# A two-block transformer kernel with its opening rebuilt: load order, first v tiles by chunks, v one tile further ahead, VectorE operations interleaved

## The chip, the cores and the metric

The kernel runs on one core of a Trainium2 chip. The metric is the device time of one execution in microseconds (us). All runs compared here are of the fast state. TensorE is called PE below, VectorE DVE, ScalarE ACT, GpSimd POOL; SP is the engine that issues most DMAs.

## The reference

Both halves take bf16 inputs; x is 2048 x 640.

```python
# A: linear attention, 32 heads of 20
qkv = layernorm(x) @ wqkv
pq, pk = q @ w_phi[h], k @ w_phi[h]
phi_q = concat(softmax(pq), softmax(-pq)); phi_k = concat(softmax(pk), softmax(-pk))
kv = phi_k^T v;  z = sum_s phi_k
o  = (phi_q @ kv) / (phi_q . z + 1e-6)
h  = x + o @ wo
# B: gated FFN, F = 1536
out = h + (gelu(layernorm(h) @ w_gate) * (layernorm(h) @ w_up)) @ w_down
```

## The kernel before

The rows are 16 tiles of 128. The opening loads x and the weights, normalizes and transposes the first tiles, and folds w_phi into the k weights ("fold": `WkT` with the block diagonal `BD` gives `Wk2`). A loop over the 16 tiles follows: `pk` = k projection on PE, `E` = exp of it on ACT (both signs), `pv` = v projection of a later tile on PE, `vS` = its copy out of PSUM on ACT, then `sk` (sums of E) and `rs` (their reciprocals) on DVE, `vt` = vS times rs, one half on POOL and the other on DVE or POOL, and at last `kvp`, the sum over tiles of E^T vt, on PE. After the loop come q, attention and FFN. The program's order on each engine is the order of the code.

```python
# opening: loads
nc.scalar.dma_start(wphi, ...)
nc.sync.dma_start(x_sb[0][:, 0:1, :], ...); nc.sync.dma_start(x_sb[0][:, 1:2, :], ...)
for u in range(2):                                   # W_v in two column halves
    nc.sync.dma_start(Wv[:, :, u * HD:(u + 1) * HD], ...)
    nc.scalar.dma_start(x_sb[0][:, 2 + u:3 + u, :], ...)
nc.sync.dma_start_transpose(WkT, A_wqkv[:, D:2 * D])
nc.scalar.dma_start(x_sb[1], ...)
nc.sync.dma_start_transpose(WqT, A_wqkv[:, 0:D])
for dst, src in ((x_sb[2], ...), (x_sb[3], ...), (Wg, wg_v)):
    nc.sync.dma_start(dst, src)
...
def k_norm(t):
    nc.vector.reduce_sum(sk, Ek[t]...)
    nc.vector.reciprocal(rs, sk)
    for s, eng in ((1, nc.gpsimd), (0, nc.gpsimd if t in VP else nc.vector)):
        eng.tensor_tensor(vt[:, s], vS[t % 6], rs[...], ALU.mult)
...
for t in range(NT):
    if 6 <= t + 5 < NT: ln_ap(t + 5, on_act=True)    # LN1T by DMA transpose
    k_tile(t)
    ...
    if t + 3 < NT: v_tile(t + 3)
    if t % 2 == 1 and t + 7 < NT: ln_st(t + 7, t + 8)
    if t in FQ: fold(WqT, Wq2, True, [FQ.index(t)])
    k_norm(t)
    if t % 2 == 1 and t >= 5: kv_tile(t - 5); kv_tile(t - 4)
    if t == 10: nc.sync.dma_start(Wo, wo_v); nc.sync.dma_start(Wu, wu_v)
    ...                                              # at t == 15: four groups of q
for t in range(12, NT): kv_tile(t)
```

The softmax here doesn't subtract the row's maximum and nothing guards it: scores larger than these inputs give would overflow.

## Time and profile before

| | before |
|---|---|
| median time when the prediction was made | 286.35 us (285.9 to 286.82, 3 runs; a fourth later makes it 286.24) |
| span of the profiled run | 284.6 us |
| PE busy / DVE busy in the span | 273.3 / 170.6 us |
| last `kvp` ends | 76.66 us |
| from there to the end of the span | 207.9 us |

The last two rows split the program where the change stops: everything that it touches lies before the last `kvp`. That end is the row's start plus its length in PE's timeline (74.94 + 1.72). A row of a timeline has start and length in us, then the engine, the source line, the operation and its tiles; a bracket gives the idle time before it and what ended that. The table of stretches of the kernel before shows the same split. Its columns are the stretch, its length, then each engine's busy us (and instructions), the granted PE clock, the DMA share and GB/s:

```profile
0.00:76.59 76.59, 70.24 (x779) 47.40 (x781) 65.72 (x108) 54.27 (x79) 50.07 (x78) 1.00 0.61 152
76.59:284.60 208.01, 203.02 (x1539) 124.67 (x1549) 104.89 (x179) 87.40 (x149) 46.86 (x131) 1.00 0.19 45
```

The first busy figure is PE's, the second that of its weight loads, the third DVE's, then ACT's and POOL's. In the first stretch PE idles for 6.35 us and DVE for 10.9, of which 6.3 lie before the first `sk` and 2.2 behind the last `vt`; in the second PE idles for 5 us in 208.

### The profile page before, as it was taken

The numbers are of one execution on the slowest core, as the hardware profiler recorded it, in microseconds if no ns is written. First come the engines' busy times: TensorE is split into PE (matmuls) and PEld (weight loads), VectorE is DVE, ScalarE is ACT, GpSimd is POOL, SyncE is SP. The second block draws the span as 40 slices with busy tenths as digits, with TensorE's granted clock in tenths as the row PEclk, the third lists the DMA queues.
The fourth block names the chain that finished last, engine by engine and source line by source line (L and its number), as shares of the span: only waits on it lengthen the run. The fifth ranks groups of instructions, "written<-read, shape, count | busy, mean of one in ns | idle before, by whom it ended". The sixth has DMA issues, their size and how long they took to land.

```text
span 284.6 us, 5745 instructions
## 1 busy us (share of the span) xinstructions
PE 273.3 (96%) x2314; PEld 172.1 (60%) x2329; DVE 170.6 (60%) x287; ACT 141.7 (50%) x227; POOL 96.9 (34%) x209
## 2 busy tenths in 40 slices
PE   7798999899999999999999999999999999999995
PEld 2475677675545678778764454675455567444573
DVE  6679999999577685775522748522575732323222
ACT  2479777965887865545425454322436440132200
POOL 6226777797501123724312144220135330000000
PEclk9999999999999999999999999999999999999999
DMA  7999622480080011314210112232021313000011
GB/s 210 230 287 299 62 51 50 98 343 1 8 273 0 0 26 25 69 48 93 48 46 25 23 25 47 47 67 73 2 46 23 59 37 92 25 1 0 0 48 46
DMA packets 40971, 21.05 MB, mean 74 GB/s; under 512 B 33136, under 2 KB 39280, under 8 KB 40944
## 3 DMA queue, kind: packets, MB, share of 16 engines
q1 hardware_dynamic: 39856, 19.67, 28.4%
q10 hardware_dynamic: 1088, 1.01, 1.1%
q8 instruction: 18, 0.29, 0.4%
q14 instruction: 9, 0.07, 0.1%
HBM read 10.18 MB, written 2.62 MB: 45 GB/s over the span
## 4 chain that ended last, share of the span: by engine, by line
PE 77%; DVE 7%; DMA 6%; ACT 4%; POOL 3%; issue 3%; ACTq 0%; DVEq 0%; POOLq 0%
PE gu L517 34%; PE pd L532 18%; PE pq L310 8%; PE po L472 7%; DMA WkT<-in_A_wqkv_dram 4%; PE pk L243 4%; PE ab L412 2%; DVE sk L272 2%; ACT E L266 2%; PE kvp L288 2%; PE pv L243 1%; POOL vt L277 1%; DVE stats L105 1%; DMA oT<-o 1%; DMA wphi<-in_A_w_phi_dram 1%
## 5 line engine op out<-in xcount | busy, mean ns | idle before, releaser
L520 ACT ACTIVATE g<-gu 128x512 bf16<-128x512 f32 (+1 forms) x60 | 30.7, 512 | 73.7 <-PE gu L517 72.8
L523 DVE TENSOR_TENSOR GT<-gu,g 128x512 bf16<-128x512 f32 (+1 forms) x60 | 34.5, 581 | 54.2 <-ACT g L520 54.0
L517 PE MATMUL gu<-LN2T,Wg 128*128 128x512 bf16 (+1 forms) x289 | 61.3, 335 | 1.5 <-DVE GT L523 0.8
L517 PE MATMUL gu<-LN2T,Wu 128*128 128x512 bf16 (+1 forms) x300 | 61.7, 336 | 0.0
L532 PE MATMUL pd<-Wd,GT 128*128 128x320 bf16 x384 | 53.9, 299 | 0.0
L532 PEld LDWEIGHTS <-GT 128*128 128x128 bf16 x384 | 37.4, 98 | 15.7 <-DVE GT L523 0.9
L517 PEld LDWEIGHTS <-Wu 128*128 128x128 bf16 x300 | 29.3, 98 | 22.6
L517 PEld LDWEIGHTS <-Wg 128*128 128x128 bf16 x300 | 28.4, 98 | 21.7 <-issue 1.0
L243 PEld LDWEIGHTS <-LN1T 128*128 128x128 bf16 x320 | 30.6, 98 | 16.1 <-DMA LN1T<-ln 1.7
L277 POOL TENSOR_TENSOR vt<-vS,rs 128x672 bf16<-128x672 bf16 x22 | 34.1, 1570 | 7.4 <-DVE rs L274 6.2
L538 DVE TENSOR_TENSOR y<-pd,x_sb 128x640 bf16<-128x640 f32 (+1 forms) x17 | 13.3, 784 | 30.7 <-PE pd L532 30.7
L420 ACT COPY AB<-ab 128x704 f32<-128x704 f32 x28 | 19.6, 748 | 14.4 <-PE ab L412 14.2
L243 PE MATMUL pv<-Wv,LN1T 128*128 128x320 bf16 x160 | 24.2, 299 | 2.5 <-DMA LN1T<-ln 1.4
L243 PE MATMUL pk<-Wk,LN1T 128*128 128x320 bf16 x160 | 24.2, 299 | 1.1 <-ACT E L266 1.0
L472 PE MATMUL po<-Wo,oT 128*128 128x320 bf16 x160 | 24.4, 299 | 0.3 <-DMA oT<-o 0.3
L453 DVE TENSOR_TENSOR tt<-AB,w 128x1280 bf16<-128x1280 f32 x16 | 23.8, 1486 | 1.2 <-POOL w L446 0.9
L266 ACT ACTIVATE E<-pk 128x640 bf16<-128x640 f32 x32 | 20.7, 702 | 5.5 <-PE pk L243 5.4
L272 DVE TENSOR_REDUCE sk<-E 128x64 f32<-128x1280 bf16 x16 | 23.1, 1447 | 0.2 <-ACT E L266 0.2
L310 PE MATMUL pq<-LN1T,Wq 128*128 128x512 bf16 x96 | 22.7, 379 | 0.2
L315 ACT ACTIVATE Eq<-pq 128x1024 bf16<-128x1024 f32 (+1 forms) x22 | 19.4, 951 | 4.7 <-PE pq L310 4.7
L472 PEld LDWEIGHTS <-oT 128*128 128x128 bf16 x160 | 15.5, 98 | 7.7 <-DMA oT<-o 0.6
L495 POOL TENSOR_SCALAR v<-sm 128x1 f32<-128x1 f32 x14 | 8.4, 599 | 30.6 <-DVE x_sb L486 30.6
(76 smaller groups left out, 260.7 us busy)
## 6 DMA issues: line engine op xcount, KB each, us to landing
out_dram<-y SPq DMA_DIRECT2D x15, 160.0 KB, 1.8
Wg<-in_B_w_gate_dram SPq DMA_DIRECT2D x1, 1920.0 KB, 11.5
Wu<-in_B_w_up_dram SPq DMA_DIRECT2D x1, 1920.0 KB, 10.5
Wd<-in_B_w_down_dram SPq DMA_DIRECT2D x1, 1920.0 KB, 7.9
x_sb<-in_A_x_dram SPq DMA_DIRECT2D x2, 640.0 KB, 5.9
Wv<-in_A_wqkv_dram SPq DMA_DIRECT2D x2, 400.0 KB, 8.0
Wo<-in_A_wo_dram SPq DMA_DIRECT2D x1, 800.0 KB, 6.3
x_sb<-in_A_x_dram ACTq DMA_DIRECT2D x1, 640.0 KB, 8.3
```

Source lines behind the costliest of these rows:

```text
L243: nc.tensor.matmul(ps[:, u, 0:HD], lhsT=lnT(t, c), rhs=W[:, c, u * HD:(u + 1) * HD], start=(c == 0), stop=(c == NC - 1))
L266: nc.scalar.activation(Ek[t][:, s, :].rearrange("p (u f) -> p u f", u=2), pk[:, :, 0:HD], ACTF.Exp, scale=(1.0 if s == 0 else -1.0))
L272: nc.vector.reduce_sum(sk, Ek[t].rearrange("p s (h f) -> p (s h) f", f=Dh), axis=AX.X)
L277: eng.tensor_tensor(vt[:, s], vS[t % 6], rs[:, s * H:(s + 1) * H, None].to_broadcast([P, H, VC]), ALU.mult)
L310: nc.tensor.matmul(pqs[j][:, i, :], lhsT=Wq2[:, kc, c * P:(c + 1) * P], rhs=LN1T[b][:, kc, :], start=(kc == 0), stop=(kc == NC - 1))
L420: (nc.vector.tensor_copy if u >= 2 - dve else nc.scalar.copy)(AB[:, :, u * UH:(u + 1) * UH].rearrange("p s h f -> p s (h f)"), ab[u][:, :, ...
L453: nc.vector.tensor_tensor(tt.rearrange("p s (h f) -> p s h f", f=Dh), num, w[:, :, :, None].to_broadcast([P, 2, H, Dh]), ALU.mult)
L472: nc.tensor.matmul(po[:, u, 0:HD], lhsT=st[t][:, c, :], rhs=Wo[:, c, u * HD:(u + 1) * HD], start=(c == 0), stop=(c == NC - 1))
L517: nc.tensor.matmul(gu[:, i, 0:n], lhsT=W[:, c, f * P:(f + 1) * P], rhs=LN2T[b][:, c, a0:a1], start=(c == 0), stop=(c == NC - 1))
L520: nc.scalar.activation(g[:, 0:n], gu[:, 0, 0:n], ACTF.Gelu_apprx_tanh)
L523: nc.vector.tensor_tensor(st[b, "g", f][:, a0:a1], gu[:, 1, 0:n], g[:, 0:n], ALU.mult)
L532: nc.tensor.matmul(pd[:, u, 0:HD], lhsT=st[b, "g", f][:, tl * P:(tl + 1) * P], rhs=Wd[:, f, u * HD:(u + 1) * HD], start=(f == 0), stop=(f ...
```

## The change

The intent: x first, W_v in row chunks so that v can start chunk by chunk; one v tile more before the first k; the big W_gate load out of the opening; DVE operations interleaved so that dependent ones do not stand next to each other.

```diff
-    VP = (1, 3, 5, 7, 9, 11)
-    FQ = (8, 9, 10, 11, 12)
+    VP = (0, 2, 4, 6, 9, 11)          # tiles whose vt is POOL's alone
+    FQ = (4, 5, 6, 7, 8)              # where W_q is folded
+    WA, WB = 2,0                      # warm-ups, before 3 and 2
+    T3 = 3                            # until here PSUM has 4 buffers, then 3 and kvp
... ln_stats: all bn_stats first, then the bn_aggr ...
+    for t in range(4):
+        (nc.sync, nc.scalar)[t % 2].dma_start(x_sb[0][:, t:t + 1, :], x_v[:, t:t + 1, :])
     nc.scalar.dma_start(wphi, ...)
-    (x tiles, W_v in column halves)
+    for c in range(NC):
+        nc.sync.dma_start(Wv[:, c, :], w_v[:, c, 2 * D:3 * D])
+    for t in (0, 2):
+        nc.sync.dma_start(x_sb[1][:, t:t + 2, :], x_v[:, 4 + t:6 + t, :])
     nc.sync.dma_start_transpose(WkT, A_wqkv[:, D:2 * D])
... x_sb[2], WqT, x_sb[3]; Wg no longer here ...
     def k_norm(t):
         nc.vector.reduce_sum(sk, ...)
+        if t - 1 in todo:
+            todo.pop(t - 1)()          # the previous tile's vt on VectorE
         nc.vector.reciprocal(rs, sk)
+        mult(1, nc.gpsimd)
+        if t in VP:          mult(0, nc.gpsimd)
+        elif t == NT - 1:    mult(0, nc.vector)
+        else:                todo[t] = lambda: mult(0, nc.vector)
... v of tiles 0 and 1 by row chunks between the transposes; v of tile 3 around the fold ...
... a first Exp on ACT ahead of all data; LN1T of tile 4 copied by DVE; ln and q moved within the loop's pass ...
-        if t + 3 < NT:
-            v_tile(t + 3)
-        if t % 2 == 1 and t + 7 < NT:
-            ln_st(t + 7, t + 8)
+        if t + 4 < NT:
+            v_tile(t + 4)
+        if t % 2 == 0 and t + 8 < NT:
+            ln_st(t + 8, t + 9)
         if t == 10:
+            nc.sync.dma_start(Wg, wg_v)
             nc.sync.dma_start(Wo, wo_v)
             nc.sync.dma_start(Wu, wu_v)
```

## The prediction

> **What bounds the kernel now.** I read the page's busy line first, then the whole list of waits of TensorE (PE), then the timelines of PE, VectorE (DVE), ScalarE (ACT), GpSimd (POOL) and the SP queue over the first 77 us, because the change touches only that stretch.
>
> The page, busy time:
> ```profile
> PE 273.3 (96%) x2314; PEld 172.1 (60%) x2329; DVE 170.6 (60%) x287; ACT 141.7 (50%) x227; POOL 96.9 (34%) x209
> ```
> PE is busy for 273.3 of 284.6 us, so only 11.3 us of PE idle exist in the whole program. The list of PE's waits says where:
> ```profile
> PE pv L243 <- DMA LN1T<-ln: 1.4, 1, 1.4
> PE wu L189 <- DVE zero L174: 1.2, 1, 1.2
> PE pv L243 <- DMA Wv<-in_A_wqkv_dram: 1.1, 1, 1.1
> PE pk L243 <- ACT E L266: 1.0, 2, 0.8
> PE gu L517 <- DVE GT L523: 0.8, 2, 0.5
> PE wa L207 <- DMA WkT<-in_A_wqkv_dram: 0.6, 1, 0.6
> ```
> The columns are us in total, times, longest. Together with four shorter waits (0.4, 0.2, 0.2, 0.2 us) the opening and the k/v loop hold 6.3 us of it. The rest of the removable time is disguised as work: 15 warm-up matmuls (`wu`), whose rows begin at 1.24, 6.23 and 7.58 us.
>
> PE is not the only engine near its limit. DVE is 9.5 to 9.7 us busy in every 10 us from 20 to 60 us. Its timeline over one pair of k tiles:
> ```profile
> 32.44 1.43 DVE L272 TENSOR_REDUCE sk<-E 128x64 f32<-128x1280 bf16 x1
> 33.97 0.55 DVE L274 RECIPROCAL rs<-sk 128x64 f32<-128x64 f32 x1
> 34.44 1.43 DVE L272 TENSOR_REDUCE sk<-E 128x64 f32<-128x1280 bf16 x1
> 35.97 0.55 DVE L274 RECIPROCAL rs<-sk 128x64 f32<-128x64 f32 x1
> 36.56 1.42 DVE L277 TENSOR_TENSOR vt<-vS,rs 128x672 bf16<-128x672 bf16 x1
> 37.90 0.87 DVE L105 BATCH_NORM_STATS2 stats<-x_sb 128x6 f32<-128x320 bf16 x2
> 38.81 0.21 DVE L106 BATCH_NORM_AGGREGATE mv<-stats 128x2 f32<-128x12 f32 x1
> 38.93 0.83 DVE L105 BATCH_NORM_STATS2 stats<-x_sb 128x6 f32<-128x320 bf16 x2
> 39.80 0.21 DVE L106 BATCH_NORM_AGGREGATE mv<-stats 128x2 f32<-128x12 f32 x1
> 39.92 1.43 DVE L272 TENSOR_REDUCE sk<-E 128x64 f32<-128x1280 bf16 x1
> ```
> Columns: start, length. A pair costs DVE 39.92 - 32.44 = 7.48 us, while PE needs about 6.4 (the first pk of three successive pairs starts at 30.44, 36.85, 43.28). DVE therefore falls behind, and is excused at the end by four q groups that fill PE:
> ```profile
> 67.28 7.73 PE L310 MATMUL pq<-LN1T,Wq 128*128 128x512 bf16 x34
> 74.94 1.72 PE L288 MATMUL kvp<-vt,E 128*64 128x84 bf16 x80
> ```
> DVE's last `vt` begins at 73.53 for 0.86 (ends 74.39), POOL's last at 73.57 for 2.00 (ends 75.57); the last kv tile needs it near 76.2. So the slack of DVE and POOL against PE is only some 0.6 us. That is the reading the prediction rests on: PE cannot gain more than 0.6 us in the opening unless DVE also ends earlier. After 77 us (q groups, attention, FFN) the kernel runs on PE with 1.5 us of idle, and the change does not reorder it.
>
> **What the Trainium skill says.** (1) "TensorE: Matmul & The Clock Gate", Part 1: PE starts at half clock, and some 3.4 us of sustained matmuls release it. The trace agrees: the first ten warm-ups take 4.31 us (431 ns each), the three at 6.23 take 0.27 each start to start. So the first ten cannot go, the other five can. (2) "DMA: Bandwidth & Descriptors", Issuing engines are not separate DMA queues: SP and ACT share 16 DMA engines. The trace agrees: the DMA share is 1.05 from 2 to 9 us (306 GB/s) and 1.09 from 9 to 14.4 (182 GB/s). Moving loads between queues brings no bandwidth; only order changes. (3) The same page, Latency and other measured facts, gives DMA transposes a lower rate (261 GB/s) than plain loads. Here still lower: 182 GB/s where WkT dominates. (4) "VectorE: DVE Perf Modes", The DRAIN you can't avoid, says that a semaphore between chained ops costs nothing extra and that each op waits until the pipe empties. This trace differs: a dependent step starts 0.10 us after the op before ended (sk to rs), an independent one 0.08 us before it ended (rs to sk). That difference is what interleaving can recover.
>
> **The change part by part.**
>
> *Loads.* x tiles 0-3 first on both queues, then W_v in five row chunks, x[4..7] behind, then WkT. Before, the first v matmul waited for a whole column half of W_v until 9.31. Ahead of chunk 0 stand only 4x160+25 KB; at 306 GB/s from about 2 us that is 4.3 us, then 0.55 us for each chunk of 160 KB: all five by about 7.3, late issues included (loads reuse eight semaphores, so the fourth chunk is issued only when an x tile has landed). The 1.1 us wait for W_v goes, and v starts when LN1T of tile 0 is copied, about 7.4. WkT, however, still has the same bytes ahead of it (2.1 MB plain) and is now behind x[4..7] on its own queue: I estimate it lands at 14.5, as before (14.42).
>
> *Warm-ups.* 3+2 become 2+0: 3 x 0.27 = 0.8 us less.
>
> *PE to the fold.* Estimated: v parts of tiles 0 and 1 from 7.4 (0.136 us a matmul), a gap of 0.5 us at 9.0 for ln of tile 2, transposes of tiles 2 and 3, done about 11.2. Then a new wait: v of tile 2 takes the PSUM buffer of v of tile 0, whose copy stands on ACT behind the LN1T copy of tile 3 (tp at 10.65, copies 0.69 each): it starts near 12.45. v2 and half of v3 (2.0 us) end near 14.5, where WkT is there. Fold, with v3's second half inside, ends about 18.0, pk0 starts about 18.3 against 17.13. But v3 (1.36) and a transpose (0.28) more are done: net 0.5 us ahead.
>
> *Loop waits on PE.* The 1.35 us wait for the LN1T transpose at 29.07 stood behind Wg (1.9 MB, 11.5 us to landing) on the queue; Wg moves to tile 10, so it goes. The waits for E (1.0 us) came from ln late for DVE's stats; stats now run 8 tiles ahead: mostly gone. Sum on PE: 0.5 + 1.35 + 1.0 = 2.9 us at most.
>
> *DVE.* Removed: per pair, vt is put between sk and rs and the aggregates behind four stats. By the start-to-start steps above a pair becomes 1.35+1.34+0.47+1.53+0.47+1.99 = 7.15 against 7.48, and a late tile 2.65 against 3.0. Added: one ln (0.4) and one LN1T copy (0.5) move from ACT. Before the first sk, DVE now also does stats of tiles 8 and 9 (2.0 us), so sk0 comes at about 22.3 against 20.01, but those 2.0 us are missing later. Walking the new order from there gives the last vt at about 71.9 against 74.39: 2.5 us earlier.
>
> *v one tile further ahead.* vS still has six buffers, so evicting v of t+4 needs vt of t-2 (before: t+3 and t-3). vt of t ends about 8 us after pk of t begins, 2.5 PE tiles. So ACT will wait for POOL and DVE, and ACT frees PSUM: a new coupling. I charge it 1 us of PE between 28 and 52 us.
>
> Sum: PE alone 2.9 less 1.0 of coupling = 1.9; DVE allows 2.5. I take **2.0 us** at the last kv tile, and the rest of the program shifts by it: 286.35 - 2.0 = 284.3 us (0.7%).
>
> **Rivals.** (a) *DVE paces the loop completely*: with six vS buffers, ACT and then PE follow vt. For it: 7.15 us a pair on DVE, 7.9 with a W_q copy, against PE's 6.4. Then the gain is what PE keeps, 0 to 1 us: 285.4 to 286.3. (b) *All idle goes*, the coupling hides behind the three PSUM buffers and the fold is not late: gain 3 to 3.5 us, 282.9 to 283.4. Against it: DVE's 2.5 us. (c) *WkT lands later*, since x[4..7] is now ahead on its queue and the transpose's issue (7.70 us before) begins only about 5.4: at 16 us the fold is 1.5 us late and the gain shrinks to 0.5 us: 285.9. (d) *A large gain above 2%* needs 5.7 us out of 6.3 us idle and 0.8 us of warm-ups in this stretch, of which the first 1.2 us before any data and most of the x latency stay: almost excluded. Slower by 2% would need a new wait of that size with PE full: hardly.
>
> **Range and chances.** 284.3, with (a) and (c) on one side and (b) on the other: 282.5 to 286.1. Faster by over 2%: 0.03; within 2%: 0.96; slower: 0.01.
>
> **What would show it.** PE's waits after: none on W_v, none on LN1T's transpose; a PE gap of about 1.2 us ahead of v of tile 2 released by ACT's vS copy; fold start near 14.5; pk0 near 18.3. DVE: sk0 near 22.3, pairs near 7.15, last vt near 71.9, with rs no longer right behind its sk in even tiles. ACT: waits of vS copies on DVE or POOL vt, which did not exist before. The last kvp should end 2 us before 76.6, and the stretch from there to the end should keep its length. Wrong would be: WkT after 15.5, PE stalls in the loop of over 2 us, or a tail that changes by over 0.5 us because of Wg's later load.

## The result

| | before | after |
|---|---|---|
| median time | 286.24 us (285.9 to 286.82, 4 runs) | 284.09 us (283.92 to 284.17, 4 runs) |
| span of the profiled run | 284.6 | 282.2 |
| last `kvp` ends | 76.66 | 72.51 |
| from there to the end | 207.9 | 209.7 |

The ratio is 0.9922, 95% interval 0.9905 to 0.994, within 2%. Ratios are the mean time of one kernel's fast runs over that of the other's of the same rounds, so not quite the ratio of the medians.

The total came out as predicted, 2.2 us less. But its two parts did not: the touched stretch gained 4.15 us, not 2.0, and the untouched rest lost 1.75 us, which was predicted to keep its length. The stretches of the changed kernel:

```profile
0.00:72.44 72.44, 68.81 (x777) 46.67 (x777) 61.13 (x110) 53.11 (x78) 48.86 (x80) 1.00 0.60 160
72.44:282.20 209.76, 203.75 (x1553) 124.75 (x1549) 104.85 (x179) 87.14 (x148) 47.08 (x131) 1.00 0.19 45
```

In the first stretch PE's idle fell from 6.35 to 3.63 us (72.44 - 68.81) and its busy time by 1.43 us (fewer and faster warm-ups, mainly): together 4.15. DVE's busy time there fell by 4.6 us. In the second stretch DVE, ACT and POOL do the same work in the same busy time.

PE's waits in the changed kernel, to be read against those in the prediction (us in total, times, longest):

```profile
PE po L511 <- DMA oT<-o: 1.8, 1, 1.8
PE tp L136 <- POOL ve L110: 1.4, 1, 1.4
PE wu L194 <- DVE zero L179: 1.2, 1, 1.2
PE gu L556 <- DVE GT L562: 0.8, 2, 0.5
PE tp L136 <- DVE ln L128: 0.5, 2, 0.3
PE pk L248 <- ACT E L280: 0.3, 1, 0.3
```

The waits for LN1T, W_v, WkT and the casts of W_k are gone from the list, which leaves out gaps under 0.15 us, and of E's 1.0 us 0.3 stay. Two have grown: the first transpose waits for the statistics of the first x tile for 1.4 us (before 0.4), and one `po` of the attention waits 1.8 us for a DMA transpose of `oT` (before 0.3). The second one is far behind the change and is the lost time of the tail.

PE's timeline in the opening of the changed kernel:

```profile
6.58 0.45 PE L136 MATMUL tp<-ident,ln 128*128 128x128 bf16 x5 [1.42 <-POOL ve L110]
...
8.04 1.94 PE L264 MATMUL pv<-Wv,LN1T 128*128 128x320 bf16 x12
...
11.95 2.20 PE L248 MATMUL pv<-Wv,LN1T 128*128 128x320 bf16 x15
13.99 0.79 PE L212 MATMUL wa<-BD,WkT 128*128 128x140 bf16 x12
...
16.83 1.57 PE L248 MATMUL pk<-Wk,LN1T 128*128 128x320 bf16 x10
```

There is no gap ahead of v of tile 2 (11.95), the fold starts at 13.99 without waiting for WkT, and the first pk at 16.83, with v of tile 3 and one transpose more already done than before.

DVE's timeline over one pair of k tiles, the counterpart of the pair in the prediction:

```profile
26.53 1.43 DVE L287 TENSOR_REDUCE sk<-E 128x64 f32<-128x1280 bf16 x1
27.88 0.85 DVE L295 TENSOR_TENSOR vt<-vS,rs 128x672 bf16<-128x672 bf16 x1
28.64 0.55 DVE L291 RECIPROCAL rs<-sk 128x64 f32<-128x64 f32 x1
29.11 1.43 DVE L287 TENSOR_REDUCE sk<-E 128x64 f32<-128x1280 bf16 x1
30.64 0.55 DVE L291 RECIPROCAL rs<-sk 128x64 f32<-128x64 f32 x1
31.11 1.61 DVE L106 BATCH_NORM_STATS2 stats<-x_sb 128x6 f32<-128x320 bf16 x4
32.63 0.33 DVE L108 BATCH_NORM_AGGREGATE mv<-stats 128x2 f32<-128x12 f32 x2
32.87 1.43 DVE L287 TENSOR_REDUCE sk<-E 128x64 f32<-128x1280 bf16 x1
```

The pair takes 32.87 - 26.53 = 6.34 us instead of 7.48. From start to start, `vt` accounts for 0.58 us of this (1.34 to 0.76), the statistics with their aggregates for 0.26, and the order of `sk`, `rs` and `vt` for 0.30. The largest single difference is `vt`: 0.85 us instead of 1.42 for the same 128x672 multiplication. All ten of them, before and then after (min/median/max in ns):

```profile
L277 DVE TENSOR_TENSOR vt<-vS,rs x10: 858/1378/1515, 22.1 to 73.5; 128x672 bf16<-128x672 bf16 x10
```

```profile
L295 DVE TENSOR_TENSOR vt<-vS,rs x10: 847/854/935, 27.9 to 69.1; 128x672 bf16<-128x672 bf16 x10
```

Before, DVE's half (36.56 to 37.98 in the pair of the prediction) fell among POOL's three multiplications (34.67 to 39.14), and both engines were slowed. Now DVE's half comes one tile later; in the pair above (27.88 to 28.73) POOL is between two groups of `vt` (one ends at 26.71, the next starts at 29.34) and runs its small operations. POOL gains too: its 22 `vt` took 34.1 us before and 29.8 after. In the loop DVE even waits for ACT (3.2 us in five waits): it is no longer the engine that falls behind.

### The profile page after: what moved, and what is told of

Same layout as the page of the kernel before. It is cut to its first block, busy times and chain, and to the rows that moved or that the text cites. A ratio compares the mean times of both kernels' runs of the same rounds, so it can differ in the third digit from the quotient of the medians.

```text
span 282.2 us, 5752 instructions
## 1 busy us (share of the span) xinstructions
PE 272.6 (97%) x2326; PEld 171.4 (61%) x2326; DVE 166.0 (59%) x289; ACT 140.2 (50%) x226; POOL 95.9 (34%) x211
## 4 chain that ended last, share of the span: by engine, by line
PE 86%; DVE 5%; ACT 3%; DMA 3%; POOL 1%; issue 1%; ACTq 0%; POOLq 0%
PE gu L556 35%; PE pd L571 18%; PE pq L335 8%; PE po L511 7%; PE pk L248 7%; PE pv L248 5%; PE kvp L313 2%; PE ab L451 2%; DVE stats L106 2%; DMA oT<-o 2%; DMA x_sb<-in_A_x_dram 1%; DVE sk L287 1%; ACT E L280 1%; ACT Eq L340 1%; PE tp L136 1%
## 5 line engine op out<-in xcount | busy, mean ns | idle before, releaser
L248 PEld LDWEIGHTS <-LN1T 128*128 128x128 bf16 x300 | 28.5, 98 | 11.8 <-issue 0.7
L295 POOL TENSOR_TENSOR vt<-vS,rs 128x672 bf16<-128x672 bf16 x22 | 29.8, 1374 | 9.1 <-DVE rs L291 7.1
L248 PE MATMUL pv<-Wv,LN1T 128*128 128x320 bf16 x140 | 21.3, 299 | 0.0
```

Source lines behind the costliest of these rows:

```text
L248: nc.tensor.matmul(ps[:, u, 0:HD], lhsT=lnT(t, c), rhs=W[:, c, u * HD:(u + 1) * HD], start=(c == 0), stop=(c == NC - 1))
L295: eng.tensor_tensor(vt[:, s], vS[t % 6], rs[:, s * H:(s + 1) * H, None].to_broadcast([P, H, VC]), ALU.mult)
```

## The experiments

All times are medians; the end of the last kvp and the tail (from there to the end of the span) are from each run's profile. "Before" runs beside each kernel on the same chip.

| run | time | ratio to before | last kvp ends | tail | wait for oT |
|---|---|---|---|---|---|
| before | 286.24 | 1 | 76.66 | 207.9 | 0.3 |
| after | 284.09 | 0.9922 | 72.51 | 209.7 | 1.8 |
| b_wg | 286.2 | 0.9992 (0.9977 to 1.0007) | 77.05 | 207.9 | 0.3 |
| b_dve | 285.08 | 0.9965 (0.9946 to 0.9983) | 75.27 | 207.9 | 0.3 |
| b_dve_wg | 284.26 | 0.993 (0.9914 to 0.9947) | 74.17 | 208.3 | 0.7 |
| a_nodefer | 285.5 | 0.9978 (0.9966 to 0.9989) | 74.44 | 209.6 | 1.8 |
| a_wgearly | 289.67 | 1.0133 (1.0112 to 1.0154) | 76.85 | 209.6 | 1.7 |
| a_x0 | 284.14 | 0.9923 (0.9904 to 0.9943) | 72.54 | 209.7 | 1.8 |
| a_tiny3 | 284.48 | 0.994 (0.9924 to 0.9955) | 73.39 | 209.5 | 1.7 |
| a_tiny20 | 283.03 | 0.9887 (0.9864 to 0.991) | 72.96 | 207.8 | none |
| a_again | 284.02 | 0.9934 (0.992 to 0.9948) | 72.82 | 209.6 | 1.7 |
| a_tiny10 | 282.33 | 0.9865 (0.9852 to 0.9877) | 72.25 | 207.9 | none |
| a_wphi | 283.19 | 0.9902 (0.9887 to 0.9917) | 72.97 | 209.5 | 1.7 |
| a_best | 282.42 | 0.9871 (0.9857 to 0.9885) | 72.39 | 207.9 | none |

All gave correct results.

### Is PE's idle worth anything while DVE lags? (b_wg, b_dve, b_dve_wg)

b_wg is the kernel before with one load moved:

```diff
-    for dst, src in ((x_sb[2], ...), (x_sb[3], ...), (Wg, wg_v)):
+    for dst, src in ((x_sb[2], ...), (x_sb[3], ...)):
...
         if t == 10:
+            nc.sync.dma_start(Wg, wg_v)
```

> The kernel before, with nothing changed but the load of W_gate, issued at tile 10 instead of in the opening. Both theories expect PE's wait of 1.35 us for an LN1T transpose at 29 us to be gone. Theory A (PE and VectorE are balanced in the k/v loop; VectorE's last vt is only 0.6 us ahead of PE): the last kvp ends at most 0.6 us earlier than 76.6, near 76.0, because the stalls for E near 50 us grow or the last kvp waits for vt; time near 285.6 us. Rival B (PE's idle counts one for one): the last kvp ends 1.35 us earlier, at 75.2; time 284.9. A late collision of one oT transpose may move either time by up to 1.6 us, so the end of the last kvp in the trace decides.

Measured: no gain at all, ratio 0.9992. The wait for LN1T is gone and others have taken its place (PE's waits in b_wg):

```profile
PE pk L243 <- ACT E L266: 1.8, 3, 0.8
PE pv L243 <- DMA Wv<-in_A_wqkv_dram: 1.5, 1, 1.5
...
PE pv L243 <- ACT E L266: 0.4, 1, 0.4
```

The waits for E grew from 1.0 to 2.2 us, about what the LN1T wait had been. (W_v happened to land 0.4 us later in this run, which makes the end of the last kvp 0.4 later. From the start of the first pk to the end of the last kvp, which leaves this out, both kernels take 59.53 us.) Rival B falls. Theory A stands, with no gain at all where it allowed up to 0.6: in the kernel before, PE's wait for LN1T cost nothing.

b_dve is the kernel before with only the DVE order: the `todo` part of `k_norm`, the grouped statistics and the new `VP` of the diff above.

> The kernel before, with the VectorE order of the changed kernel alone (vt of odd tiles put off until after the next tile's sum, statistics grouped, GpSimd taking both halves of tiles 0, 2, 4, 6, 9, 11). Theory C (the deferred vt no longer runs beside GpSimd's vt, and so takes 0.85 us instead of 1.4): vt on VectorE has a median near 0.86 us, a pair of tiles takes 6.4 us on VectorE instead of 7.48, the last vt ends near 70 us. Rival D (only the hand-over gaps between dependent operations go): vt stays near 1.4 us and a pair takes 7.15. In time: PE loses its 1.0 us of waits for E but keeps the LN1T wait, so the last kvp ends 0.8 to 1.0 us earlier (near 75.7), time near 285.4.

Measured: 1.0 us faster (285.08), last kvp 1.4 us earlier. DVE's ten `vt` take 1.04 us on average instead of 1.20 (some, as those at 40.6 and 47.5 us, still meet POOL's and take 1.38), POOL's 22 take 29.3 us instead of 34.1, and the last `vt` ends at 71.71, not at the 70 expected, because DVE now waits for E and once, for 1.23 us, for a fold on PE. A pair takes 6.4 to 7.0 us with those waits. Theory C holds in the main, rival D's 7.15 with 1.4 for every vt does not. The gain on PE is larger than expected; 0.6 us of it are shorter waits for W_v and WkT, which landed earlier in this run.

> Both of the two above in the kernel before. Theory A: the two gains add to more than the sum of the single ones, since W_gate's wait counts in full only once VectorE is out of the way: the last kvp ends near 74.2 (2.35 us earlier), time near 284.0 unless a late collision takes some back. Rival B: W_gate's 1.35 us come on top of the other one's gain only as they did alone.

Measured: 284.26, 2.0 us faster, last kvp 2.5 us earlier. Alone the two were worth 0.2 +- 0.4 (from the interval) and 1.0 us; together 2.0. On the times alone the surplus over the sum, 0.8 us, is no larger than its uncertainty (an estimate from the three intervals: 0.8). The traces decide: from the first pk to the last kvp the loop is shorter by 0 in b_wg, 0.78 in b_dve and 1.84 us in both (59.53, 59.53, 58.75 and 57.69). W_gate's move is worth 1 us once DVE is out of the way and nothing before that. This is also as fast as the whole change (0.993 against 0.9922): two edits of some twenty lines carry the measured gain. That the rebuilt opening adds another 1.7 us at the last kvp (74.17 against 72.51) does not show in the total, since the tail takes most of it back (1.4 us). Which of the other edits in the opening and the loop make these 1.7 us, no run separates.

### Undoing the deferral in the changed kernel (a_nodefer)

```diff
-            todo[t] = lambda: mult(0, nc.vector)
+            mult(0, nc.vector)
```

> The changed kernel with one thing undone: vt of the odd tiles runs on VectorE at once behind its reciprocal instead of one tile later. Theory C: vt on VectorE goes back to 1.3 to 1.5 us for the tiles of the loop and GpSimd's to over 1.4, a pair takes 7.1 us or more on VectorE, the last vt ends near 72.5 instead of 69.9, GpSimd and VectorE make PE wait, and the last kvp ends 1 to 2 us later than 72.4. Rival E (the opening's gain alone made the difference): the last kvp stays within 0.3 us of 72.4.

Measured: 285.5, so 1.4 us slower than the change (on another chip; each against its own kernel before, 0.9978 and 0.9922), and the last kvp 1.93 us later. Of these, 0.44 lie ahead of the first pk (17.27 against 16.83), where nothing was changed. Rival E falls. Theory C came true in part: the pairs of DVE take 7.21 and 7.45 us where the change takes 6.34 and 7.07, POOL's 22 `vt` take 34.3 us, and the last `vt` ends at 72.83. But only the first two of DVE's ten `vt` are slow (1.27 and 1.41 us). The other eight take 0.86: they start just before POOL's, and POOL's bears the delay. And the wait that is new on PE in the loop is not one for `vt` (a row of PE's timeline, and one of the chain of work that ended last, with start and length):

```profile
34.82 1.53 PE L248 MATMUL pv<-Wv,LN1T 128*128 128x320 bf16 x10 [1.09 <-DMA LN1T<-ln]
30.34 4.43 DMA LN1T<-ln
```

This transpose took 4.43 us from issue to landing, where most of the loop take 2.4, and a fetch of PE's instructions began 1.18 us behind its issue: the collision that the section on the tail below describes. So this run does not separate the worth of the deferral from such a collision, which makes 1.09 of the 1.49 us by which the loop is longer. For DVE's order alone, b_dve stands: 1.0 us.

The trace before and this run agree with the Trainium skill ("GPSIMD Engine Reference", Specifications), which says that GpSimd's interface to SBUF is shared with VectorE and contends with VectorE instructions of two SBUF inputs. In both traces the one that started second bore most of the delay: 128x672 bf16 took 0.86 us on DVE when it began first and 1.27 to 1.51 when POOL was already multiplying, 1.31 us on POOL when it began first and 1.90 to 2.00 when DVE was at it.

### W_gate early in the changed kernel (a_wgearly)

```diff
     nc.sync.dma_start(x_sb[3], x_v[:, 12:16, :])
+    nc.sync.dma_start(Wg, wg_v)
...
         if t == 10:
-            nc.sync.dma_start(Wg, wg_v)
```

> The changed kernel with W_gate's load moved back into the opening, behind x tiles 12 to 15. My reading: W_gate (1.9 MB) stands ahead of the LN1T transposes of tiles 6 to 8 and lands near 29 us; PE needs tile 6 at 24, one v tile earlier than the kernel before, so it waits 3 to 5 us where that one waited 1.35; VectorE catches up meanwhile, so the last kvp ends 1.5 to 3.5 us later than 72.4. Rival: as in the kernel before, the wait is absorbed by VectorE's lag, and the last kvp moves by less than 0.5 us.

Measured: 289.67, slower than the kernel before; in the profile (its fastest run, 288.1) the last kvp is 4.3 us later than in the change, with this wait:

```profile
PE pv L249 <- DMA LN1T<-ln: 3.1, 1, 3.1
```

My reading holds for the wait (3 to 5 us expected); the effect at the last kvp is larger than the 1.5 to 3.5 expected. With v one tile further ahead PE meets the blocked queue earlier: it could have started this v at 24.05 us, against 27.72 for the waiting v in the kernel before. That the two parts of the change need each other fits this; it was not tested further. Part of the loss is in the clock: the granted clock was 0.988 to 0.994 in these runs against 0.998 to 1.0 in the change, and in the profile it was 0.92 and 0.91 from 20 to 30 and from 30 to 40 us, where the pk right behind the wait took 2.87 us instead of 1.52. No run here shows why.

### Where the tail's 1.75 us went (a_tiny3, a_tiny10, a_tiny20)

Behind the last kvp, PE waits longer than before at one place of the changed kernel's timeline:

```profile
137.04 1.53 PE L511 MATMUL po<-Wo,oT 128*128 128x320 bf16 x10 [1.85 <-DMA oT<-o]
```

The transpose was issued at 132.60 and landed 4.4 us later; the median of all oT transposes is 2.6. The trace's DMA packets around it (counted from the trace; a transpose has 672 packets; 16 increments of its semaphore release PE):

```
                     oT issued  its packets move              PE-instruction packet, 16 KB   increments
after                132.60     665 at 133.8-134.8,            134.87 for 0.88 us             136.88-137.00
                                7 at 135.7-135.95
a_tiny10             132.33     672 at 133.5-134.45            132.13 for 1.06 us             134.75-134.90
before               136.75     672 at 137.9-139.2             137.09 for 0.95 us             139.45-139.58
```

A packet of 16 KB on a queue of its own recurs once per some 250 rows of PE (matmuls and weight loads; 180 to 320) throughout the program, and is of the kind that the page of the profile calls "instruction". I take it for a fetch of PE's instructions; the runs below, in which it moves with PE's rows, bear this out. In the changed kernel one of them starts at 134.87, when seven packets of the transpose are still to come; these move only when it is done, from 135.7. The Trainium skill ("DMA: Bandwidth & Descriptors", Queues, rings and completion order) says that each DMA engine takes turns between its queues a whole packet at a time; the trace agrees, one packet of 0.88 us holding up seven. If that is the cause, moving the fetch along PE's program moves the wait. Small matmuls, whose result nobody uses, were put where PE idles anyway, behind the first warm-ups:

```diff
     warm(NWARM)
+    for _ in range(n):        # n = 3, 10, 20
+        nc.tensor.matmul(wu[:, 0, 0:32], lhsT=zero[:, 0:P], rhs=zero[:, 0:32], start=True, stop=True)
```

> The changed kernel with three matmuls of 32 columns (result unused) put behind the first ten warm-ups, where PE idles for 1.4 us anyway. They give PE as many instructions as in the kernel before (4660 rows; the change has 4654), so that the 16 KB fetches of PE's instructions fall on other work. Theory F (the new 1.85 us wait for an oT transpose at 137 us comes from such a fetch, which starts at 134.9 just as the transpose's last packets move): the opening and the last kvp (72.4) stay, the wait falls to 0.3 to 0.7 us, the stretch from the last kvp to the end shrinks from 209.8 to 208.0 to 208.5, time 282.5 to 283.0. Rival G (the late loads of W_gate, W_o and W_up or another part of the change lengthen the tail): the wait and the stretch stay, time 284.1.

Measured: a miss. With three the fetch still started 2.0 us after the issue of the transpose (135.5 and 133.47), the wait stayed at 1.7 and the tail at 209.5. Having as many PE instructions as the kernel before does not bring the fetch back to its old place. (The first statistics started 0.26 us later in this run and a 0.4 us wait for LN1T appeared, so the last kvp was 0.9 us later too. That transpose had met a fetch as well: it took 3.43 us instead of 2.4.)

> As the run with three, but twenty such matmuls (40 rows of PE, some 1.3 us, still inside the first wait of 1.4 us). Theory F: the fetch falls some 36 rows (about 2 us of PE work) earlier than in the change, so at 132.5 to 133, ahead of the transpose's data at 133.8; wait at most 0.3 us at that transpose, though another transpose may meet another fetch; time 282.4 to 283.0. Rival G: time 284.1.

Measured: as theory F expected, with the fetch 0.7 us earlier than said. It came at 131.8, before the transpose's issue at 133.04; no wait for oT, tail 207.8, time 283.03.

> Ten small matmuls (20 rows), between the run with three (wait 1.7 us, fetch 2.0 us after the issue of the oT transpose) and the one with twenty (no wait, fetch 1.2 us before it). Theory F: the fetch falls near the transpose's issue or within its transfer, as in the kernel before (0.35 us after the issue, wait 0.3); the wait is between 0 and 1.0 us, time 282.9 to 283.6. Rival H (it is the number of small matmuls, by some other path, that shortens the tail): the tail shrinks in proportion, by about 0.9 us, with the wait at 0.9.

Measured: the fetch at 132.13, 0.2 us before the issue; no wait, tail 207.9, time 282.33, below the 282.9 to 283.6 expected. The same place of PE's timeline as above:

```profile
134.95 1.53 PE L513 MATMUL po<-Wo,oT 128*128 128x320 bf16 x10
```

Between three and ten the wait goes from 1.7 to none at once. Rival H (in proportion) falls, and rival G too, since all loads stayed where the change has them. So the tail's loss is a collision in time between an instruction fetch and one transpose, and the change caused it only by shifting PE's instruction stream. b_dve_wg (fetch 0.3 us after the issue) has a wait of 0.7, the kernel before (0.3 us) one of 0.3.

All fourteen traces bear this out. Of their 392 transposes of `oT` and `LN2T`, 22 took over 4.0 us, and in each a fetch had begun 0.97 to 2.32 us behind the issue. The 363 without a fetch between 0.8 and 2.35 us behind the issue took at most 3.46 (median 2.57). In a_tiny10 and a_tiny20 the fetch hit the `oT` transpose ahead of this one instead (4.73 and 4.27 us), and PE waited for neither, as it had other work until then. So a collision costs something only where PE has nothing else to do, and moving the fetches can also make a new one: the waits for LN1T in a_tiny20 and a_best (0.8 us each) stand behind transposes that took 3.57 and 3.61 us with a fetch 1.1 to 1.2 us behind their issue.

What stays open: all 16 increments of the delayed transpose came 0.93 us after its last packet, against 0.3 in the undelayed one. The Trainium skill ("DMA: Bandwidth & Descriptors", Why a DMA increments its semaphore by 16 and not by 1) says that the engines finish independently and that the semaphore counts them; this explains a late increment of the one engine that was held up, not of all sixteen. Both kinds occur here: of the transpose of 4.73 us in a_tiny10, 15 increments came at 118.83 to 119.02 and one at 121.14. No run here separates this.

### The first x tile (a_x0, a_wphi)

The first statistics, which wait for the first x tile, start at 3.94 in the change and at 3.30 in the kernel before.

```diff
 a_x0:
-        (nc.sync, nc.scalar)[t % 2].dma_start(x_sb[0]...)
+        (nc.sync, nc.sync, nc.scalar, nc.scalar)[t].dma_start(x_sb[0]...)
 a_wphi: the same queues, and w_phi issued ahead of the x tiles on ACT
```

> The changed kernel with x tiles 0 and 1 on SP and 2 and 3 on ACT, as before, where the change alternates the queues. In the change the first x tile landed 0.64 us later than before (3.94 against 3.30), with two tiles starting at once. If two tiles at the same moment are the reason, the first statistics start at 3.3 to 3.5, PE's first wait falls from 1.42 to about 0.8 us, and the last kvp ends 0.5 us earlier (71.9); time 283.6 if the oT wait stays. If the time to landing is set by something else, nothing moves.

Measured: nothing moved (3.89; 284.14). PE's first wait did fall, to 0.85, but only because the warm-ups ended at 5.69 instead of 5.16; the first transpose starts at 6.54 as against 6.58. The run was badly chosen: tile 2 on ACT now starts together with tile 0, so that it doesn't test the theory.

> The changed kernel with the loads that lie ahead of W_v as in the kernel before: w_phi first on ACT, x tiles 2 and 3 behind it, tiles 0 and 1 on SP, so that only tile 0 and w_phi's 25 KB start at 0.79 us. The run that only swapped the queues left two x tiles starting together and moved nothing. If two tiles at one moment are the reason for the late landing, the first statistics start at 3.3 instead of 3.9, PE's first wait falls to about 0.4 to 0.8 us, and the last kvp ends 0.4 to 0.6 us earlier; time 283.5 with the oT wait in place. If not, 284.1.

Measured: the statistics start at 3.20 instead of 3.91 (a_again), the first transpose at 5.84 instead of 6.55, and the median to 283.19 against 284.02 of the unchanged kernel on the same chip. But the runs fall into two groups, 282.9 to 283.4 and 284.1 to 284.2. The profiled run is of the slower one: there the fold waits 0.6 us for WkT, which has become the next bound of the opening, and the last kvp is no earlier than in a_again. This agrees with two tiles starting at one moment as the reason for the late landing; that the gain at the end then depends on WkT is argued from this one profile.

### The control and the best version (a_again, a_best)

> The changed kernel once more, unchanged, so that the next three have it on their own chip. Expected: ratio 0.992 to 0.993, the 1.8 us wait for oT at its place, the last kvp within 0.5 us of 72.4.

Measured: as expected, 284.02, ratio 0.9934, wait for oT 1.7.

> The two together: loads as in the run before this and twenty small matmuls. Expected 282.4 us, ratio 0.987, faster than both kernels: last kvp near 71.9, no wait for oT, 207.9 us from there to the end. If the small matmuls no longer fit into the shorter first wait (20 of them take 0.7 to 1.3 us), 282.9.

Measured: 282.42, ratio 0.9871, as expected. It beats both kernels, but not a_tiny10 (282.33, 0.9865), whose interval overlaps; w_phi first brings nothing measurable on top. The last kvp came at 72.39, not 71.9; the wait for LN1T named above is the likely reason. The smallest edit that beats both kernels by 1.7 and 3.8 us is therefore the changed kernel with ten idle matmuls. This margin lies in where the fetches fall, so it is one of this program alone. Against the unchanged change on the same chip it is 0.9865 / 0.9934 = 0.993.

## Why the prediction was right or wrong

The time, 284.3 predicted and 284.09 measured, lies well inside the range. It does so because two errors nearly cancel: 2.15 us too little gain up to the last kvp, and 1.75 us of loss behind it that the prediction excluded. By its own steps:

- **What bounds the kernel**: right, and shown. PE could not gain unless DVE ended earlier (b_wg), and could when it did (b_dve_wg). The 1.5 us of PE idle after 77 us were misread: the table of stretches has 5.0 there, since the list of waits leaves out short gaps.
- **Loads**: the wait for W_v went as predicted. v started at 8.04, not 7.4, because x landed 0.64 us later, which the prediction took as unchanged; a_wphi gives the likely reason. WkT landed at 13.8 (6.96 + 6.8 to landing), not 14.5. The 261 GB/s that the prediction takes from the Trainium skill ("DMA: Bandwidth & Descriptors", Latency and other measured facts) are that page's figure for a non-contiguous middle dimension; for the contiguous case it gives 350 to 400, and no run here separates the two.
- **Warm-ups**: 0.27 us start to start is the length of the row over three. The starts lie 0.22 apart (6.23, 6.45, 6.66), so three fewer are 0.65 us, not 0.8.
- **PE to the fold**: mis-sized, 0.5 us predicted and 1.9 measured. The new wait ahead of v of tile 2 did not exist (11.95 with no gap, while ACT's copy of tile 0 began only at 12.47). The prediction took the PSUM buffers to rotate; of the four, only that of tile 2's transpose had been copied by then (10.72 to 11.41, the one of tile 3 from 11.88), so v must have got this one. The fold with v's second half then took 2.7 us (13.99 to 16.69), not 3.5. So the first pk came at 16.83, not 18.3: 0.3 us earlier than before, with 1.64 us of other work done.
- **Loop waits on PE**: right for LN1T (1.35 us gone), and nearly for E (0.7 of 1.0 gone).
- **DVE**: right direction, too small. The pair was put at 7.15 us with vt at 1.34 start to start; it took 6.34 with vt at 0.76 and the statistics with aggregates at 1.76 instead of 1.99. The prediction counted hand-over gaps and missed that both engines' vt slowed each other, though a vt of 0.86 stood in the trace that it read (where DVE began before POOL). The first sk came at 20.66, not 22.3, the last vt ended at 69.94, not 71.9.
- **The coupling by six vS buffers**: the mechanism exists (ACT waited for DVE's vt three times, 1.5 us), its size on PE does not: PE waited once in the loop, 0.28 us for E, which is the rest named above, and not 1.
- **The sum**: 2.0 us predicted at the last kvp, 4.15 measured. The terms as measured, 1.94 to the fold, 1.35 for LN1T and 0.7 for E, make 4.0. Against the prediction's, the opening was put 1.4 too low and the coupling charged 1.0 too much, while E gave 0.3 less: 2.1 of the 2.15 us missing.
- **The tail**: wrong. It was to keep its length, and the prediction named a change of over 0.5 us "because of Wg's later load" as what would refute it. It grew by 1.75, not by that load but by a fetch that lies in no row of any engine. That this cancelled most of the surplus ahead of it, and so brought the total to within 0.3 us of the forecast, was luck.
- **Rivals**: (b) came closest for the stretch, and even it stopped at 3 to 3.5 us. (a) and (c) did not happen; (d) was rightly almost excluded.

## What to carry to other kernels

When two engines are balanced, removing a wait from one of them does nothing until the other ends earlier; look at both ends before costing an edit. An operation that one engine does in very different times may be slowed by a neighbour: in the pair shown, moving it by one iteration was worth 0.58 us on DVE, as much as the other changes of order together (0.56). And split a result at the point where the change ends: a total that fits can hide two errors.

## What the Trainium skill lacked or had wrong

- "VectorE: DVE Perf Modes", The DRAIN you can't avoid: says, from copies, that a semaphore between chained operations costs nothing extra. Here a dependent operation started 0.10 us after the end of the one before, an independent one 0.08 us before it. The section itself says that an operation that is not held starts earlier; what it lacks is the size, 0.18 us between the two.
- "DMA: Bandwidth & Descriptors": gives no cost for fetches of an engine's instructions beside other transfers. Here 16 KB packets of 0.88 to 1.8 us, one per some 250 rows of PE, share the DMA engines, and a transpose with one beginning 0.95 to 2.25 us behind its issue took 3.6 to 4.7 us instead of 2.6.
